# Fewer places for the second products of attention, and a later split of one expert's weights

## The chip, the cores and the metric

The kernel runs on one core of a Trainium2 chip. The metric is the device time of one launch in microseconds (us). TensorE (PE) multiplies, VectorE (DVE), ScalarE (ACT) and GpSimd (POOL) work element by element, and SyncE (SP) issues DMAs. Each engine runs its own instructions in the order in which the program wrote them, and semaphores make it wait for others.

## The reference, cut to what matters

```python
# attention: 4 batches, 8 heads, 576 positions, head size 64, a bias from a small MLP of distances
scores = q @ k.T / 8 + bias                  # softmax over keys
attn   = exp(scores - max) / (sum + 1e-9)
x      = attn @ v                            # 2304 tokens of 512
# dense layer, rational activation
h = x @ w_in                                 # 512 -> 2048
g = (a0 + a1*h + a2*h2 + a3*h3) / (1 + |b0|*|h| + |b1|*h2 + 1e-6)
x = g @ w_out                                # 2048 -> 512
# 8 experts, each token to the best one
e = argmax(x @ w_gate + modality_bias[modality])
out[token] = gate * (relu(x @ w1[e]) @ w2[e])    # 512 -> 1024 -> 512
```

## The kernel before, in words

**Attention.** The work goes by units of one pair of heads and one batch: 16 units of nine steps, 144 steps `g = 9u + j`, in one loop (L524 to L584). A step works on one tile of 128 queries (the ninth takes the 64 left over of both heads) against 576 keys. Its parts are written one after another, each for another tile, so that a tile passes through the loop in about five steps:

- `expo(g-2)` (L351, ACT): the exponentials, with their sum; `recip(g-3)` (L363, L364, DVE, and L366, POOL): the reciprocals of the sums of two tiles;
- the list `pend` (L546 to L548): what copies PSUM of the step before to SBUF, namely `stack_evac` (L302 to L311: the transposed q and k of the next unit), `rest_evac` and `av_evac` (L445, DVE: the result of a unit's second product, times the reciprocals);
- `trans_pe(g-4)` (L393, PE): four transposes of exponentials (L396 and L397 add two in every second step), and `trans_evac` (L370, ACT);
- `scores(g)` (L330, PE): four products of 288 columns (eight in step 8) into one of two PSUM places named sc;
- `stack_pe` (L289 to L294, PE), in steps 0, 1, 2, 3 and 7;
- the second products `attn @ v` (`av_pe`, L436, PE): two output halves (256 and 320 queries), each of five chunks of keys. The tables `AV0` and `AV1` (L520, L521) say at which steps of the next unit they stand: half 0 in steps 0, 1 and 2, half 1 in steps 4, 6, 7 and 8. Each chunk is done on 64 columns of the array for each of the two heads;
- `rowmax(g-1)` (L346, DVE): adds the bias, writes the sum to SBUF and keeps the row's extreme. It frees the PSUM place that `scores(g+1)` writes.

A conversion of the dense layer's weights runs beside it (`CONV`, L516).

**Dense layer.** Six tiles of 384 tokens, each with 16 chunks of the hidden size: 96 iterations G (L1125). In each, PE does 12 first products (L671) and 12 second products (L759, five iterations behind); ACT and DVE compute the rational function of two chunks at a time (L635 to L664). The results of a tile are copied out of PSUM (L766, L768) in the next tile, and its tokens are routed: logits (L775), choice (L785, L787), a chain of small DVE operations (L805 to L853), a place in each expert's table, and three scatters from POOL into tables in DRAM (L863).

**The first expert.** When the last tile begins (G = S1 = 80) the counts of five tiles already name an expert with many tokens. Its weights come as 16 pieces of 128x512. Each piece is loaded (`wa_load`) and split into a high and a low part: a cast on ACT (L937) and a subtraction on POOL (L938). One piece is split in each of the iterations 82 to 97. Behind the last tile (G = 96 to 100) PE does the second products that are left, transposes the rows of 384 early tokens of that expert (`block_x`, L1038) and begins its first products (`split_h`, L1055, eight groups). Then the last tile is copied out and routed, `split_h` goes on, `split_y` (L1076) does the expert's second products, and further rows are gathered by the tables that the last scatters have filled.

The lines that set the order around the change:

```python
AV0 = {0: (0, 1), 1: (2,), 2: (3, 4)}
AV1 = {4: (0, 1), 6: (2,), 7: (3,), 8: (4,)}
i = G - S1 - 2
if 0 <= i < 16:
    wa_tile(i)
    wa_split(i, spec[i], nc.gpsimd)
```

Of the kernel before, what the change touches and what calls it, by code (L numbers as in the profile page):

```python
# [8 lines left out]
F32 = mybir.dt.float32  # L9
F32R = mybir.dt.float32r  # L10
# [4 lines left out]
ALU = mybir.AluOpType  # L15
# [73 lines left out]
def attention(ctx, tc, k, ins):  # L89

    nc = tc.nc
# [5 lines left out]
    pst, xq = k.pst, k.xq  # L97
# [5 lines left out]
    bp = bctx.enter_context(tc.tile_pool(name="bp", bufs=1, side="right"))  # L103
# [336 lines left out]
    def av_evac(u, n):  # L440
        r = units[u]
        w = Q1 if n == 0 else S - Q1
        if n == 0:
            r.xs = ap.tile([P, S], F32, name="xs")
        nc.vector.tensor_tensor(r.xs[:, n * Q1:n * Q1 + w], r.av[:, 0:w], r.aR[n][:, 0], ALU.mult)  # L445
        if n == 1:
            later[g + (3 if u < NU - 1 else 1)] = lambda: nc.sync.dma_start(k.xT[r.p, r.b], r.xs)
# [38 lines left out]
    for s in range(37):  # L486
# [18 lines left out]
        if s in (8, 11, 14, 17, 20):  # L505
            i = (4, 0, 1, 2, 3)[(s - 8) // 3]
# [10 lines left out]
            5: [(1, 1), (8, 0)], 6: [(7, 0), (3, 1), (2, 1), (0, 2)], 7: [(4, 1)], 8: [(5, 1)]}  # L517
    STACK = {0: 4, 1: 0, 2: 1, 3: 2, 7: 3}
    SPLIT = {6: (0,), 7: (1,), 8: (2, 3)}
    AV0 = {0: (0, 1), 1: (2,), 2: (3, 4)}  # L520
    AV1 = {4: (0, 1), 6: (2,), 7: (3,), 8: (4,)}  # L521
    pend = []
    setup = routing_setup(tc, k, ins)
    for g in range(NG + 6):  # L524
        u, j = divmod(g, 9)
# [7 lines left out]
        w, i = divmod(g - 2, 9)  # L533
# [5 lines left out]
            next(setup)  # L539
        if g in later:  # L540
            later[g]()
        if 0 <= g - 3 < NG:
            recip(g - 3)
        if 0 <= g - 2 < NG:
            expo(g - 2)
        for f in pend:  # L546
            f()
        pend = []  # L548
        if 0 <= g - LAG < NG:
            trans_pe(g - LAG)  # L550
            trans_evac(g - LAG)
# [5 lines left out]
        if u + 1 < NU and j in STACK:  # L557
            i = STACK[j]
            ps = stack_pe(u + 1, i)
            pend.append(lambda u=u, i=i, ps=ps: stack_evac(u + 1, i, ps))  # L560
        if 0 <= u - 1 < NU - 1 and j in AV1:
            for c in AV1[j]:
                av_pe(u - 1, 1, c)
            if j == 8:
                pend.append(lambda u=u: av_evac(u - 1, 1))
        if 0 <= g - 1 < NG:
            rowmax(g - 1)
# [3 lines left out]
        v = u - 1  # L571
        if 0 <= v < NU and j in AV0:
            for c in AV0[j]:
                av_pe(v, 0, c)
# [12 lines left out]
        n = g - NG  # L587
# [87 lines left out]
def moe(ctx, tc, k, ins, x2_d, out):  # L675

    nc = tc.nc
# [3 lines left out]
    bp = bctx.enter_context(tc.tile_pool(name="bp1", bufs=2, reuse_waits="tile"))  # L681
    wop = k.persist.enter_context(tc.tile_pool(name="wop", bufs=16, side="right", reuse_waits="tile"))
    pb, xq = k.pst, k.xq
# [184 lines left out]
    w1, w2 = ins["moe2_w1"], ins["moe2_w2"]  # L868
# [51 lines left out]
        k.meta = c0.tile([P, 3, NE], I32, name="meta")  # L920
        nc.vector.tensor_copy(k.meta, mf)

    wa = {}

    def wa_tile(i):
        wa[i] = k.wip.tile([P, 2, DM], F32R, name="w_a", bufs=16)

    def wa_load(i, raw, e):
        if i < 8:
            src = w1[bass.ds(e, 1), (i // 2) * P:(i // 2 + 1) * P, (i % 2) * DM:(i % 2 + 1) * DM]  # L930
        else:
            src = w2[bass.ds(e, 1), (i - 8) * P:(i - 7) * P, :]
        nc.sync.dma_start(raw, src.rearrange("o p n -> (o p) n"))

    def wa_split(i, raw, eng):
        w = wa[i]
        nc.scalar.copy(w[:, 0], raw)  # L937
        eng.tensor_tensor(w[:, 1], raw, w[:, 0].bitcast(F32), ALU.subtract)  # L938


    wsets, rowsets, colsets, halves = [], [], [], []
# [159 lines left out]
            nc.gpsimd.indirect_dma_start(out, bass.IndirectOffsetOnAxis(ap=r.tl[:, a:a + 1].bitcast(U32), axis=0),  # L1101
                                         y, None, bounds_check=NT - 1, oob_is_err=False)

    spec = {}

    def spec_raw(i):

        j = i % 6
        if j == 0:
            a = bp.tile([P, 3, DM], F32, name="x", bufs=1)  # L1110
            k.sraw = [a[:, n] for n in range(3)]
        elif j == 3:
            a = xq.tile([P, 2, DM], F32, name="kn")
            k.sraw = [a[:, n] for n in range(2)]
        elif j == 5:
            k.sraw = [xq.tile([P, DM], F32, name="qn")]
        spec[i] = k.sraw.pop(0)
        wa_load(i, spec[i], k.e0)

    tiles[0] = k.x0  # L1120
    NG = NTT * NF
    FULL = 10
    S1, S0 = NG - NF, NG - NF + 9

    for G in range(NG + 5):  # L1125
        t, f = divmod(G, NF)
# [60 lines left out]
            pick()  # L1187
        if G == S1:
            k.e0 = nc.sync.value_load(k.pick[0:1, 0:1], min_val=0, max_val=NE - 1)
        for i in {1: range(6), 5: (6, 7, 8), 7: (9, 10, 11), 11: (12, 13, 14), 12: (15,)}.get(G - S1, ()):  # L1190
            spec_raw(i)
        i = G - S1 - 2
        if 0 <= i < 16:
            wa_tile(i)
            wa_split(i, spec[i], nc.gpsimd)
        if G == S0 - 1:
            head()
        if G == S0:
# [53 lines left out]
    a = rt.tile([P, 4, NB], F32, name="x2", bufs=1)  # L1252
    for p in range(2):
        c = K()
# [295 lines left out]
```

## Time and profile before

| | us |
|---|---|
| median of three runs | 1071.61 (1068.4 to 1072.78) |
| the profiled execution, its own time | 1070.2 |
| its span, first to last instruction | 1068.4 |
| attention's steps at their steady pace | from about 80 to 375 |
| the dense layer's six tiles | from about 377 to 802 |
| the last tile's end and the first expert's early tokens | about 802 to 870 |

The trace shows every instruction with its start and duration. PE's products overlap, so that a product's duration is longer than the time it costs: what a group costs is read from the start of one group to the start of the next. In brackets stands how long the engine was idle before an instruction, and what ended that.

### The profile page before, as it was taken

The page shows a single profiled execution, that of the slowest core. Times are in us where ns is not written, and L with a number is a line of the kernel's source. Part 1 is how long each engine was busy: PE and PEld are TensorE (multiplying, and loading weights), DVE is VectorE, ACT ScalarE, POOL GpSimd, SP SyncE. Part 2 cuts the span into 40 slices and gives each one's busy share as a digit, 9 for nine tenths or more (in the row PEclk, how much of TensorE's full clock was granted, in tenths as well). Part 3 has the DMA queues.
Part 4 walks back from the last instruction along what each step waited for, and adds up shares of the span by engine and source line. Part 5 has one row for each costly group of instructions (what it writes and reads, how often), then busy time and mean ns, then how long its engine had stood idle before and what let it go on. Part 6 is the DMA issues. An engine that isn't in the chain of part 4 may idle for free. (4 is left out here: it accounts for less than half of the span.)

```text
span 1068.4 us, 19126 instructions
## 1 busy us (share of the span) xinstructions
PE 1017.6 (95%) x6804; PEld 885.4 (83%) x6804; DVE 754.4 (71%) x1544; ACT 651.0 (61%) x1283; POOL 280.8 (26%) x449
## 2 busy tenths in 40 slices
PE   6989999999999999999999999999986999999995
PEld 4667777777777779999999999999885889999983
DVE  7988998888888858898888988888886312111210
ACT  6878778877877857666667766676664222222221
POOL 3433343443443310202112021031253142211210
PEclk9999999999999999999999999999998999999998
DMA  5886885774664236105103031051131256411100
GB/s 170 299 269 165 232 242 182 212 225 128 177 181 116 92 108 260 30 1 30 31 1 38 23 23 38 1 30 60 60 70 30 23 145 230 140 42 40 50 31 18
DMA packets 122074, 113.36 MB, mean 106 GB/s; under 512 B 65055, under 2 KB 94495, under 8 KB 121952
## 3 DMA queue, kind: packets, MB, share of 16 engines
q1 hardware_dynamic: 117828, 101.53, 35.6%
q0 software_dynamic: 3728, 10.25, 3.1%
q8 instruction: 61, 1.00, 0.4%
q14 instruction: 61, 0.50, 0.2%
q10 hardware_dynamic: 396, 0.08, 0.0%
HBM read 78.09 MB, written 33.79 MB: 105 GB/s over the span
## 5 line engine op out<-in xcount | busy, mean ns | idle before, releaser
L759 PE MATMUL sc<-gh,w_b 128*128 128x384 f32 x752 | 209.7, 340 | 3.3 <-ACT x L766 3.3
L759 PEld LDWEIGHTS sc<-gh,w_b 128*128 128x128 f32 x752 | 139.3, 190 | 4.1 <-ACT x L766 3.9
L759 PE MATMUL sc<-gl,w_b 128*128 128x384 f32 x376 | 127.7, 340 | 0.0
L393 PEld LDWEIGHTS tr<-idf,e 128*128 128x128 f32 x576 | 80.5, 207 | 49.3 <-issue 24.9
L351 ACT ACTIVATE e<-e,st 128x576 f32<-128x576 f32 x144 | 112.2, 779 | 13.3 <-DVE st L346 11.4
L370 ACT COPY aT<-tr 128x512 f32<-128x512 f32 x144 | 84.4, 586 | 44.8 <-PE tr L393 42.9
L346 DVE CUSTOM_DVE_ANT_0 e<-sc,bias_s 128x576 f32<-128x576 f32 x144 | 107.6, 748 | 5.4 <-PE sc L330 4.1
L1065 DVE SCALAR_TENSOR_TENSOR hl<-tr,hh 128x256 fp32r<-128x256 f32 x56 | 23.8, 424 | 121.5 <-ACT hh L1064 121.1
L671 PE MATMUL tr<-kn,w_a 128*128 128x384 f32 x372 | 107.3, 343 | 2.1 <-DVE t L642 2.0
L393 PE MATMUL tr<-idf,e 128*128 128x128 f32 x576 | 104.6, 304 | 1.7 <-DVE kk L311 0.9
L330 PE MATMUL sc<-kk,qS 128*128 128x288 f32 x512 | 99.1, 315 | 0.7 <-DVE st L346 0.7
L660 ACT CAST gh<-t 128x768 fp32r<-128x768 f32 x47 | 39.3, 835 | 89.2 <-DVE t L656 89.2
L436 PE MATMUL av<-aT,vn 128*64 128x320 f32 (+1 forms) x512 | 82.8, 424 | 0.0
L1055 PE MATMUL tr<-kn,w_a 128*128 128x256 f32 x448 | 81.6, 280 | 0.9 <-ACT w_b L1100 0.7
L330 PEld LDWEIGHTS sc<-kk,qS 128*128 128x128 f32 x512 | 73.0, 191 | 2.2 <-DVE st L346 1.0
L671 PEld LDWEIGHTS tr<-kn,w_a 128*128 128x128 f32 x372 | 68.0, 188 | 5.7 <-DVE t L642 3.2
L759 PEld LDWEIGHTS sc<-gl,w_b 128*128 128x128 f32 x376 | 71.5, 190 | 0.0
L1055 PEld LDWEIGHTS tr<-kn,w_a 128*128 128x128 f32 x448 | 69.7, 188 | 1.7 <-ACT w_b L1100 1.1
L863 POOL DMA_INDIRECT tab<-ids,si x18 | 21.2, 1178 | 189.7 <-DVE cum L859 167.9
L1076 PE MATMUL sc<-w_a,hh 128*128 128x512 f32 x224 | 70.9, 393 | 0.0
L366 POOL TENSOR_SCALAR rb<-st 128x128 f32<-128x128 f32 x80 | 23.8, 298 | 171.5 <-DVE st L364 154.2
L654 DVE SCALAR_TENSOR_TENSOR t<-t,coef,r 128x768 f32<-128x768 f32 x47 | 49.3, 1048 | 23.9 <-ACT r L650 23.9
(303 smaller groups left out, 2533.2 us busy)
## 6 DMA issues: line engine op xcount, KB each, us to landing
bias_d<-bo SPq DMA_DIRECT2D x36, 295.5 KB, 2.9
kn<-in_k_dram SPq DMA_DIRECT2D x64, 128.0 KB, 3.4
cst<-in_moe_w_out_dram SPq DMA_DIRECT2D x16, 512.0 KB, 4.1
wo_d<-cvw SPq DMA_DIRECT2D x16, 512.0 KB, 2.8
cst<-in_moe_w_in_dram SPq DMA_DIRECT2D x16, 512.0 KB, 4.0
w_b<-wo_d SPq DMA_DIRECT2D x16, 512.0 KB, 6.4
w_b<-in_moe_w_dram SPq DMA_DIRECT2D x16, 512.0 KB, 8.2
x_d<-xr SPq DMA_DIRECT2D x18, 256.5 KB, 9.7
```

Source lines behind the costliest of these rows:

```text
L330: nc.tensor.matmul(ps[:, hf, 0:HF], st, mv[:, hf * HF:(hf + 1) * HF], start=n == 0, stop=n == last)
L346: nc.vector.tensor_tensor_reduce(out=ev, in0=ps[:, :, 0:HF], in1=bv, scale=-1.0, scalar=3.0e38, op0=ALU.add, op1=ALU.min, accum_out=st[:, ...
L351: nc.scalar.activation(e, e, AF.Exp, bias=st[:, 0:1], scale=-1.0, accum_out=st[:, 1:2])
L370: nc.scalar.copy(dst, src)
L393: nc.tensor.transpose(ps[:, c * P:(c + 1) * P], both[:, e0 + c % 2:e0 + 2 * P:2], k.idf)
L436: nc.tensor.matmul(r.av[64 * hd:64 * hd + 64, 0:w], st, mv, start=c == 0, stop=c == 4)
L654: nc.vector.scalar_tensor_tensor(q.t, q.t, co[:, 0:1], q.r, ALU.add, ALU.mult)
L660: self.nc.scalar.copy(gh, q.t)
L671: nc.tensor.matmul(h[:, 0:k.NB], k.wi[f][:, wv, dc * P:(dc + 1) * P], xv[dc], start=n == 0, stop=n == 11)
L759: nc.tensor.matmul(r.acc[dc][:, 0:NB], wo[f][:, wv, ws], gv, start=f == 0 and n == 0, stop=f == NF - 1 and n == 2)
L1055: nc.tensor.matmul(ps[:, 0:n], w[:, wv, cs], xv[dc // 2][:, dc % 2], start=j == 0, stop=j == 11)
L1076: nc.tensor.matmul(r.acc[a], r.h[f][hv][:, cs], wa[8 + f][:, wv], start=f == 0 and n == 0, stop=f == 7 and n == 2)
```

## The change

In attention the second products of a unit stand in four places instead of seven: half 0 in steps 0 (three chunks) and 2 (two), half 1 in steps 4 (two) and 6 (three). The copy `av_evac` of half 1 follows step 6. The list `pend` runs ahead of `recip` and `expo` in each step.

In the dense layer four pieces of the expert are split in iterations 85, 88, 91 and 94, and the other twelve in iterations 98, 99 and 100, four in each, behind the last token tile's products. The order of the pieces is changed so that the four needed by the first four `split_h` come first. Pieces 8 to 15 are loaded into places of the dense layer's second weights, w_b, as these come free, instead of waiting for the places of earlier pieces.

```diff
-    AV0 = {0: (0, 1), 1: (2,), 2: (3, 4)}
-    AV1 = {4: (0, 1), 6: (2,), 7: (3,), 8: (4,)}
+    AV0 = {0: (0, 1, 2), 2: (3, 4)}
+    AV1 = {4: (0, 1), 6: (2, 3, 4)}
...
+        for f in pend:
+            f()
+        pend = []
         if 0 <= g - 3 < NG:
             recip(g - 3)
         if 0 <= g - 2 < NG:
             expo(g - 2)
-        for f in pend:
-            f()
-        pend = []
...
-            if j == 8:
+            if j == 6:
                 pend.append(lambda u=u: av_evac(u - 1, 1))
...
+    def wa_split(i):
+        w = wa[i] = k.wip.tile([P, 2, DM], F32R, name="w_a", bufs=16)
+        nc.scalar.copy(w[:, 0], raw[i])
+        nc.gpsimd.tensor_tensor(w[:, 1], raw[i], w[:, 0].bitcast(F32), ALU.subtract)
...
+    WORD = (0, 2, 4, 6, 1, 3, 5, 7) + tuple(range(8, 16))
+    SPLITS = {5: WORD[0:1], 8: WORD[1:2], 11: WORD[2:3], 14: WORD[3:4], 18: WORD[4:8], 19: WORD[8:12], 20: WORD[12:16]}
...
-        for i in {1: range(6), 5: (6, 7, 8), 7: (9, 10, 11), 11: (12, 13, 14), 12: (15,)}.get(G - S1, ()):
-            spec_raw(i)
-        i = G - S1 - 2
-        if 0 <= i < 16:
-            wa_tile(i)
-            wa_split(i, spec[i], nc.gpsimd)
+        if G == S1 + 1:
+            wa_first()
+        if S1 + 6 <= G < S1 + 10:
+            wa_second(G - S1 - 6)
+        if G == S1 + 12:
+            wa_rest()
+        for i in SPLITS.get(G - S1, ()):
+            wa_split(i)
```

PE in steps 6, 7 and 8 of a unit, before: L393 are the transposes of exponentials, L330 the scores, L291 the transposes of k, L436 the second products (two rows a chunk, one for each head).

```order
L330 MATMUL sc<-kk,qS_1034 128x288 x4
L436 MATMUL av<-aT_1209,vn 64x320 x2
L393 MATMUL tr<-idf,e 128x128 x4
L396 MATMUL av<-idf,e 128x128
L397 MATMUL av<-idf,rb 128x128
L330 MATMUL sc<-kk,qS_1035 128x288 x4
L291 MATMUL tr<-idf,kn 128x128 x4
L436 MATMUL av<-aT_1209,vn 64x320 x2
L393 MATMUL tr<-idf,e 128x128 x4
L330 MATMUL sc<-kk,qrem_119 128x288 x8
L436 MATMUL av<-aR_1210,vrem_117 64x320 x2
L393 MATMUL tr<-idf,e 128x128 x4
```

The same place in the changed kernel:

```order
L330 MATMUL sc<-kk,qS_1034 128x288 x4
L436 MATMUL av<-aT_1209,vn 64x320 x4
L436 MATMUL av<-aR_1210,vrem_117 64x320 x2
L393 MATMUL tr<-idf,e 128x128 x4
L396 MATMUL av<-idf,e 128x128
L397 MATMUL av<-idf,rb 128x128
L330 MATMUL sc<-kk,qS_1035 128x288 x4
L291 MATMUL tr<-idf,kn 128x128 x4
L393 MATMUL tr<-idf,e 128x128 x4
L330 MATMUL sc<-kk,qrem_119 128x288 x8
L393 MATMUL tr<-idf,e 128x128 x4
```

The chunks of steps 7 and 8 stand in step 6, and steps 7 and 8 keep nothing but transposes and scores.

DVE from step 8 to step 0 of the next unit, before: L363 and L364 are the reciprocals, L310 and L311 empty the PSUM of the transposes of k, L346 is `rowmax` (of step 7, then of step 8), L445 the copy of half 1.

```order
L363 TENSOR_SCALAR st<-st 128x2
L364 RECIPROCAL st<-st 128x2
L310 CAST kk<-tr 128x512
L311 TENSOR_TENSOR kk<-tr,kk 128x512
L346 ISA e,st<-sc,bias_s 128x576
L346 ISA st 128x1
L76 CAST cvw<-cvt 128x512
L445 TENSOR_TENSOR xs<-av,aR_1210 128x320
L346 ISA e_1533,st<-sc,bias_s 128x576
```

The same place in the changed kernel:

```order
L310 CAST kk<-tr 128x512
L311 TENSOR_TENSOR kk<-tr,kk 128x512
L363 TENSOR_SCALAR st<-st 128x2
L364 RECIPROCAL st<-st 128x2
L346 ISA e,st<-sc,bias_s 128x576
L346 ISA st 128x1
L76 CAST cvw<-cvt 128x512
L346 ISA e_1536,st<-sc,bias_s 128x576
```

The reciprocals stand between the emptying of PSUM and `rowmax`, and L445 is gone from here (it stands in step 7).

ACT behind the last token tile, before: L1041 copies the transposed early rows, L1064 is the ReLU of `split_h`, L937 a piece's cast, L766 the copy of the last tile out of PSUM.

```order
L1041 CAST w_b<-av 128x384
L1064 ACTIVATE w_b<-tr 128x384
L937 CAST w_a<-kn 128x512
L1064 ACTIVATE w_b<-tr 128x384
L766 COPY x_9942<-sc 128x384 x2
```

The same place in the changed kernel (its lines are numbered 1063, 1086, 936 and 767):

```order
L1063 CAST w_b<-av 128x384
L1086 ACTIVATE w_b<-tr 128x384 x2
L936 CAST w_a<-kn 128x512
L936 CAST w_a<-qn 128x512
L936 CAST w_a<-x 128x512 x2
L936 CAST w_a<-w_b 128x512 x8
L767 COPY x_9942<-sc 128x384 x2
```

Twelve casts stand ahead of the last tile's copy, and on POOL the twelve subtractions stand in the same way ahead of the last tile's three scatters.

## Rows read from the trace of the kernel before

**Rows 1.** Busy time by stretch: PE, PEld, DVE, ACT, POOL, clock, DMA, GB/s.

```profile
200.00:225.00 25.00, 25.00 (x187) 19.22 (x186) 21.98 (x62) 20.65 (x47) 9.21 (x20) 1.00 0.74 221
```

**Rows 2.** Timeline of PE, steps 0 to 4 of a unit: start, duration, instruction.

```profile
199.92 0.77 PE L330 MATMUL sc<-kk,qS 128*128 128x288 f32 x4
...
200.79 1.08 PE L436 MATMUL av<-aT,vn 128*64 128x256 f32 x8
...
202.31 0.77 PE L330 MATMUL sc<-kk,qS 128*128 128x288 f32 x4
...
203.31 0.65 PE L436 MATMUL av<-aT,vn 128*64 128x256 f32 x4
...
204.61 0.77 PE L330 MATMUL sc<-kk,qS 128*128 128x288 f32 x4
...
207.27 0.77 PE L330 MATMUL sc<-kk,qS 128*128 128x288 f32 x4
...
208.86 0.77 PE L330 MATMUL sc<-kk,qS 128*128 128x288 f32 x4
```

**Rows 3.** Timeline of PE, the scores of steps 5 to 8 and 0.

```profile
211.51 0.77 PE L330 MATMUL sc<-kk,qS 128*128 128x288 f32 x4
...
212.51 0.77 PE L330 MATMUL sc<-kk,qS 128*128 128x288 f32 x4
...
214.62 0.77 PE L330 MATMUL sc<-kk,qS 128*128 128x288 f32 x4
...
216.96 1.30 PE L330 MATMUL sc<-kk,qrem 128*128 128x288 f32 x8
...
219.60 0.77 PE L330 MATMUL sc<-kk,qS 128*128 128x288 f32 x4
```

**Rows 4.** Timeline of DVE in the same unit, steps 4 and 8.

```profile
208.53 0.16 DVE L363 TENSOR_SCALAR st<-st 128x2 f32<-128x2 f32 x1
...
208.81 0.74 DVE L346 CUSTOM_DVE_ANT_0 e<-sc,bias_s 128x576 f32<-128x576 f32 x1
...
215.87 0.69 DVE L310 CAST kk<-tr 128x512 fp32r<-128x512 f32 x1 [0.62 <-PE tr L291]
...
217.20 0.75 DVE L346 CUSTOM_DVE_ANT_0 e<-sc,bias_s 128x576 f32<-128x576 f32 x1
```

**Rows 5.** Timeline of PE, first product of iterations 68, 79, 84 and 95.

```profile
672.38 0.34 PE L671 MATMUL tr<-kn,w_a 128*128 128x384 f32 x1
...
721.67 0.34 PE L671 MATMUL av<-kn,w_a 128*128 128x384 f32 x1
...
742.74 0.34 PE L671 MATMUL tr<-kn,w_a 128*128 128x384 f32 x1
...
800.33 0.44 PE L671 MATMUL tr<-kn,w_a 128*128 128x384 f32 x1 [1.17 <-DVE t L642]
```

**Rows 6.** PE's groups by line, 800 to 823.3 us: busy, mean ns, idle before.

```profile
L1055 PE MATMUL tr<-w_b,w_a 128*128 128x384 f32 x12 | 3.5, 416 | 4.1 <-ACT w_b L1041 3.7 <-DVE w_b L1042 0.4
L1038 PE MATMUL av<-idf,qs 128*128 128x128 f32 x8 | 1.9, 300 | 3.8 <-DVE w_b L1042 2.5 <-DVE t L642 1.1
```

**Rows 7.** Timeline of DVE in iteration 97.

```profile
815.97 2.11 DVE L654 SCALAR_TENSOR_TENSOR t<-t,coef,r 128x768 f32<-128x768 f32 x1
818.12 1.02 DVE L655 SCALAR_TENSOR_TENSOR r<-q,one,r 128x768 f32<-128x768 f32 x1
```

**Rows 8.** Groups of the split pieces on ACT and POOL, 735 to 830 us.

```profile
L937 ACT CAST w_a<-x 128x512 fp32r<-128x512 f32 x9 | 5.6, 617 | 0.0
...
L938 POOL TENSOR_TENSOR w_a<-x,w_a 128x512 fp32r<-128x512 f32 x9 | 13.6, 1516 | 36.8 <-ACT w_a L937 29.5 <-PE av L1038 4.0 <-PE sc L759 3.3
```

**Rows 9.** Timeline of PE and POOL behind the last tile.

```profile
833.61 2.26 PE L1055 MATMUL tr<-w_b,w_a 128*128 128x384 f32 x12
...
843.96 1.01 POOL L863 DMA_INDIRECT tab<-ids,si  x1 [18.05 <-DVE count L856]
...
866.20 0.98 PE L1038 MATMUL av<-idf,xg 128*128 128x128 f32 x7 [1.05 <-DMA xg<-x_d,tixg]
```

More of the change, by code (lines that the diff above doesn't have):

```diff
@@ L921, in order, with wa_load, wa_first, wa_rest @@
         nc.vector.tensor_copy(k.meta, mf)
[L923 to L928, printed above, removed]
+    wa, raw = {}, {}
+    def wa_load(i, place):
         if i < 8:
-            src = w1[bass.ds(e, 1), (i // 2) * P:(i // 2 + 1) * P, (i % 2) * DM:(i % 2 + 1) * DM]
+            src = w1[bass.ds(k.e0, 1), (i // 2) * P:(i // 2 + 1) * P, (i % 2) * DM:(i % 2 + 1) * DM]
         else:
[L932 to L938, printed above, removed]
+            src = w2[bass.ds(k.e0, 1), (i - 8) * P:(i - 7) * P, :]
+        raw[i] = place
+        nc.sync.dma_start(place, src.rearrange("o p n -> (o p) n"))
+    def wa_split(i):
+        w = wa[i] = k.wip.tile([P, 2, DM], F32R, name="w_a", bufs=16)
+        nc.scalar.copy(w[:, 0], raw[i])
+        nc.gpsimd.tensor_tensor(w[:, 1], raw[i], w[:, 0].bitcast(F32), ALU.subtract)
+    def wa_first():
+        a = bp.tile([P, 3, DM], F32, name="x", bufs=1)
+        b = xq.tile([P, 2, DM], F32, name="kn")
+        c = xq.tile([P, DM], F32, name="qn")
+        for i, place in zip(WORD, (a[:, 0], a[:, 1], a[:, 2], b[:, 0], b[:, 1], c)):
+            wa_load(i, place)
+    def wa_rest():
+        a = bp.tile([P, 3, DM], F32, name="x", bufs=1)
+        for n in range(2):
+            wa_load(WORD[6 + n], a[:, n])
+    def wa_second(n):
+        a = wop.tile([P, 2, DM], F32, name="w_b", bufs=16)
+        for j in range(2):
+            wa_load(8 + 2 * n + j, a[:, j])
+    WORD = (0, 2, 4, 6, 1, 3, 5, 7) + tuple(range(8, 16))
+    SPLITS = {5: WORD[0:1], 8: WORD[1:2], 11: WORD[2:3], 14: WORD[3:4], 18: WORD[4:8], 19: WORD[8:12], 20: WORD[12:16]}
     wsets, rowsets, colsets, halves = [], [], [], []
@@ L1102, in block_out @@
                                          y, None, bounds_check=NT - 1, oob_is_err=False)
[L1104 to L1118, printed above, removed]
     tiles[0] = k.x0
```

## The prediction

> **What bounds the kernel now.** I read the busy time by stretch first. In a steady stretch of attention PE is never idle, DVE is busy for 21.98 of 25 us and ACT for 20.65 [rows 1]. PE being busy proves little, since its products overlap, so I went on to PE's timeline of one unit and took times from start to start. From the scores of step 0 to those of the next unit's step 0 it takes 219.60 - 199.92 = 19.68 us [rows 2, 3], and most units repeat this. In these rows hardly any group of PE waits for a semaphore: it is PE's order that costs time, and what to look for is which of its entries cost more than their columns. In the dense layer I compared the last tile with the one before, iteration by iteration, on PE; then I read who ended PE's waits behind it, and last the way from the final scatters to the rows that they let PE have.
>
> **Attention: the price of a place.** A chunk of 256 columns costs 1.08 - 0.65 = 0.43 us (two chunks against one in a place) [rows 2]; one of 320 columns I take as 0.43 x 320/256 = 0.54.
> - Step 1. Scores to scores takes 2.30 us with one chunk in between (202.31 to 204.61) and 1.59 us in step 3, where the same transposes stand without a chunk (207.27 to 208.86) [rows 2]. The place costs 0.71, its chunk 0.43, so 0.28 is the price of entering and leaving.
> - Step 7. Without a chunk and without other transposes the interval is 1.00 (211.51 to 212.51) [rows 3]. Step 3's 1.59 exceeds this by 0.59 for six transposes, of which the four of the stack get 0.43. Step 7 takes 2.34 (214.62 to 216.96) [rows 3]: 2.34 - 1.00 - 0.43 - 0.54 = 0.37.
> - Step 8. It takes 2.64 (216.96 to 219.60) [rows 3]. Four more score products are half of the 1.00, two transposes the remaining 0.16 to 0.20 of the 0.59: 2.64 - 1.00 - 0.50 - 0.20 - 0.54 = 0.40.
>
> Three places less are worth 0.28 + 0.37 + 0.40 = 1.05, taken as 1.0 us a unit for PE. The chunks that move add no boundary where they go, since a place stands there already.
>
> **What is late next.** Scores of step 0 need the PSUM place that `rowmax` of step 7 frees. In the trace that `rowmax` ends at 217.20 + 0.75 = 217.95, and the scores start at 219.60: 1.65 us to spare [rows 3, 4]. `rowmax` cannot come earlier, because it stands behind L310, and L310 waits for PE's transposes of k in step 7 (0.62 us idle before it) [rows 4]. From those transposes on PE loses the chunks of steps 7 and 8 with their boundaries, 2 x 0.54 + 0.37 + 0.40 = 1.85. The new order also puts the reciprocals between L311 and `rowmax`, 0.28 (208.53 to 208.81) [rows 4]. So 1.65 - 1.85 - 0.28 = -0.48: PE waits about 0.45 in step 0 of each unit. Elsewhere I find nothing late: L445 leaves step 0, and steps 0 and 6 grow by 0.43 and 1.08 for the others to catch up. ACT gets its PSUM copies ahead of the exponentials; in 19.7 us it idles 3.4 (4.35 of 25) [rows 1], and a copy made sooner also frees the place of PE's transposes sooner. The result's DMA follows L445 by three steps as before, on an SP queue with nothing urgent behind it. A wait on SP or POOL is not added.
>
> 15 units lose 1.0, 14 pay 0.45: 15.0 - 6.3 = **8.7 us**. The ends: 15 (no new wait) and 0 (DVE takes everything).
>
> **The last tile.** Iterations 84 to 95 take 800.33 - 742.74 = 57.6 us; the same stretch of the tile before takes 721.67 - 672.38 = 49.3 [rows 5]. The 8.3 us more go with the 16 splits. A subtraction on POOL holds up a DVE operation that has two inputs in SBUF: L654 took 2.11 where the next, of the same size, took 1.02 [rows 7]. With four splits in place of fourteen up to iteration 95, about 0.9 of such a delay falls on every three iterations, within what DVE idles. I let 0.9 of the 8.3 stay (the counts and the `head` chain are still there): 7.4 gained; ends 4 and 8.3.
>
> From 800 to 823.3 PE idles 4.1 + 3.8 = 7.9 us before the early rows' transposes and the first `split_h` [rows 6]. This is one chain through ACT and DVE for the last pair of chunks; three subtractions lengthen it by 1.09 each and three casts by 0.5 each (0.617 [rows 8], overlapping its neighbour), 4.8 together. That much I take off; ends 0 and 7.9. 7.4 + 4.8 = 12.2 us by which the second products of the last tile end sooner.
>
> **What the moved splits cost.** Call M the end of these products (833.61 before [rows 9]). Two groups of twelve products stand between the second `split_h` and M, an iteration's worth, so the casts begin at about M - 4. Twelve take 12 x 0.52 = 6.2, to M + 2.2; two copies of the last tile follow on ACT, 0.8, and the logits, which PE had at M + 2.2 (behind `split_h`), begin at M + 3.4: 1.2 late. The subtractions take 12 x 1.5 = 18 [rows 8], from M - 3.5 to M + 14.5. Meanwhile the routing chain has five operations with two inputs in SBUF; each can lose between nothing and a whole subtraction, 1.5, and I take 0.72, 3.6 together. The scatters were issued at 843.96 = M + 10.35 [rows 9]; now they need the chain, M + 10.35 + 1.2 + 3.6 = M + 15.2, and POOL free at M + 14.5. So they are issued 4.8 late against M. The rows that hang on them released PE 866.20 - 843.96 = 22.2 us after the first scatter [rows 9], and PE had only just come to wait for them (1.05 idle). So PE goes on 4.8 later against M, and this stretch gains 12.2 - 4.8 = **7.4 us**. The ends: 0 lost (12.2) and 10 lost (2.2: the subtractions at 2 us each, as much as the DVE operation beside one took [rows 7]).
>
> The Trainium skill, page "SBUF — State Buffer", section "Who interferes with whom", says that a DVE instruction with two SBUF inputs contends with a GpSimd instruction that reads SBUF, and that the loser fully blocks until the other ends. The row of 2.11 us agrees. By the rule alone each of the five operations would lose nearly a whole subtraction, 7.2 us instead of 3.6, and the time would be 3.6 higher; this is the third rival.
>
> Pieces 1, 3, 5 and 7 are needed by the fifth `split_h`, behind logits and two groups of products, some 6 us after M, and are split by M + 2.5; pieces 8 to 15 by M + 14.5, their first product comes after M + 17. Their loads wait only for places that PE has left five iterations before.
>
> **Sum.** 1070.2 - 8.7 - 7.4 = 1054.1 by the profiled execution's own time (its span is 1068.4). The median of the runs shown is 1.4 higher, 1071.61; so 1055.5, taken as 1055.
>
> **The rivals.**
> 1. DVE does not become late: PE keeps the whole 15 us. For it: 1.65 us to spare where I count 2.13 as used, so a small error decides; against it: L310's wait, which ties `rowmax` to PE's own transposes. 1055.5 - 6.3 = 1049.
> 2. The boundary's price goes with the chunks and not with the place, so that attention gains nothing and the change does not do what it says there. For it: that price rests on differences between steps; against it: three steps give 0.28 to 0.40. 1055.5 + 8.7 = 1064.
> 3. POOL's queue: subtractions of 2 us and a routing chain blocked in full. Scatters then wait until M + 20 or more. 1055.5 + 5 = 1060.5.
> 4. The other side: ACT. Three times in a unit a copy of the stack now stands ahead of an exponential. If ACT has run ahead of PE, that copy is not ready and ACT waits for up to a step, 2.30 [rows 2], where it did an exponential before. 3 x 2.30 = 6.9, less 3.4 that ACT idles anyway, less the 1.0 gained: +2.5 a unit, 15 x 2.5 - 7.4 = +30, so 1102. It decides once ACT loses more than 3.4 + 1.0 + 0.5 a unit. Against it: ACT's copies already follow PE's step closely, and the exponentials have two steps before they are needed.
>
> **Chances.** The forecast 0.58, rival 1 0.14, rival 2 0.08, rival 3 0.16, rival 4 0.04. The range: the forecast's own, from the ends of its terms, is about 1050 to 1060; with rivals 1 and 3 and part of 2 it is 1046 to 1063. Half a per cent (5.4 us) is about what a measurement of this kernel can tell from no change. Forecast and rivals 1 and 3 lie beyond it on the fast side, rival 2 too, but close: faster 0.91, same 0.05, slower 0.04.
>
> **What would show it.** In attention: four groups of second products a unit; score intervals of 1.6 in step 1, 1.4 in step 7 and 1.8 in step 8; a unit of 19.1 to 19.2 us; in step 0 a PE that waits 0.4 to 0.5 for `rowmax`. 18.7 would be rival 1, 19.7 rival 2, ACT busy without a gap and units over 20 rival 4. In the dense layer: the last tile's iterations at the pace of the tile before; a PE idle of about 3 us in place of 7.9 behind it; twelve casts in a row ahead of L766's copy; scatters some 15 us after the end of the second products; PE waiting again before the transposes of gathered rows. I am wrong in the main if the unit's length does not fall below 19.4, or if the scatters come no sooner than before.

## Result and profile after

The changed kernel takes 1083.18 us (median, 1082.04 to 1086.29), the kernel before, run beside it, 1070.57 (1068.4 to 1072.78): ratio 1.0125, 95% interval 1.01 to 1.015. It is slower by 12.6 us where 1055 was forecast. The profiled execution has a span of 1081.6 us at a mean granted clock of 0.990 of full speed.

The loss lies in attention alone. Iteration 66 of the dense layer starts at 683.12 us instead of 664.03, 19.1 later; from there to the end the changed kernel is 5.9 us shorter. First the stretch of attention that answers to [rows 1]: PE, which had no gap, now has 1.5 us of gaps in 25. DVE and ACT are busy for a smaller share, but a unit takes longer: in a steady unit DVE is busy for 18.42 us of 21.20, where it was 16.89 of 19.68.

```profile
200.00:225.00 25.00, 23.52 (x174) 18.30 (x174) 21.08 (x53) 19.35 (x45) 10.51 (x19) 1.00 0.67 206
```

Next, PE's timeline of the changed kernel from step 7 of one unit to step 1 of the next; it answers to [rows 2, 3], with columns as there.

```profile
226.22 0.77 PE L330 MATMUL sc<-kk,qS 128*128 128x288 f32 x4
...
227.67 1.31 PE L330 MATMUL sc<-kk,qrem 128*128 128x288 f32 x8
...
229.88 0.79 PE L330 MATMUL sc<-kk,qS 128*128 128x288 f32 x4
...
231.38 0.28 PE L294 MATMUL tr<-idr,qs 128*128 128x128 f32 x1 [0.59 <-POOL qs L268]
231.59 1.51 PE L436 MATMUL av<-aT,vn 128*64 128x256 f32 x12
...
233.53 0.77 PE L330 MATMUL sc<-kk,qS 128*128 128x288 f32 x4
234.37 0.54 PE L289 MATMUL tr<-idr,qs 128*128 128x128 f32 x4
235.62 0.75 PE L393 MATMUL tr<-idf,e 128*128 128x128 f32 x4 [0.70 <-ACT aT L370]
```

Read from scores to scores, as in the prediction, a steady unit looks like this (us; "forecast" is the sum of the prediction's terms for each step). Of the 14 units that follow the first, 12 take 21.12 to 21.26 and two 21.60 and 23.48; in the kernel before ten take 19.68 and four 20.17 to 20.77.

| step | 0 | 1 | 2 | 3 | 4 | 5 | 6 | 7 | 8 | unit |
|---|---|---|---|---|---|---|---|---|---|---|
| before | 2.39 | 2.30 | 2.65 | 1.59 | 2.65 | 1.00 | 2.12 | 2.34 | 2.64 | 19.68 |
| forecast | 2.82 | 1.59 | 2.65 | 1.59 | 2.65 | 1.00 | 3.20 | 1.43 | 2.25 | 19.18 |
| after | 3.65 | 2.81 | 2.66 | 1.59 | 2.65 | 1.00 | 3.19 | 1.44 | 2.21 | 21.20 |

Seven of the nine steps came out within 0.04. Steps 0 and 1 are 0.83 and 1.22 too long, and that is the whole miss in a steady unit. The bracketed waits in PE's rows name two releasers: in step 0 POOL's split of q (L268, the part of the split that PE's transposes L294 read), in step 1 ACT's copy of the transposed exponentials (L370). POOL's timeline of the changed kernel at that place:

```profile
229.32 0.30 POOL L366 TENSOR_SCALAR rb<-st 128x128 f32<-128x128 f32 x1 [4.57 <-DVE st L364]
229.58 1.74 POOL L268 TENSOR_TENSOR qs<-qt,qs 128x320 fp32r<-128x320 f32 x2
231.28 0.73 POOL L78 TENSOR_TENSOR cvw<-cvt,cvw 128x256 fp32r<-128x256 f32 x1
```

POOL had nothing to do for 4.57 us, because the broadcast of the reciprocals (L366) stood at the head of its queue and waited for DVE; the two pieces of q's split (L268), for which nothing was missing, stood behind it and ended 0.06 before PE's L294 started. DVE's timeline of the same stretch shows why L366 was late and what followed:

```profile
227.47 0.69 DVE L310 CAST kk<-tr 128x512 fp32r<-128x512 f32 x1
...
229.00 0.17 DVE L364 RECIPROCAL st<-st 128x2 f32<-128x2 f32 x1
229.08 0.74 DVE L346 CUSTOM_DVE_ANT_0 e<-sc,bias_s 128x576 f32<-128x576 f32 x1
...
229.74 0.99 DVE L76 CAST cvw<-cvt 128x512 fp32r<-128x512 f32 x1
...
231.33 0.97 DVE L61 TENSOR_SCALAR cvt<-cst 128x512 uint32<-128x512 uint32 x1
232.33 1.11 DVE L62 SCALAR_TENSOR_TENSOR cvt<-cst,cvt 128x512 uint32<-128x512 uint32 x1
...
233.67 0.29 DVE L303 TENSOR_TENSOR kk<-tr,kk 128x128 fp32r<-128x128 f32 x1
```

The rows answer to [rows 4]: the reciprocal now stands behind both copies of k's stack. L76 and L61 take more than twice the 0.42 us that each takes before, with POOL's displaced L268 and L78 running beside them; with L62 (1.11 in place of 0.69) that is the 1.5 us that DVE is busy for longer in a unit. The small stack (the transposes of the last 64 keys and queries, step 0) is copied by L302 and L303, last in this queue; they are late, and with them ACT, whose timeline closes the chain:

```profile
234.06 0.27 ACT L305 CAST qrem<-tr 128x128 fp32r<-128x128 f32 x1 [2.28 <-DVE st L363]
234.22 0.78 ACT L351 ACTIVATE e<-e,st 128x576 f32<-128x576 f32 x1
...
234.99 0.57 ACT L370 COPY aT<-tr 128x512 f32<-128x512 f32 x1
```

ACT idles 2.28 us in front of L305. This copy empties the same PSUM place as L303 and waits for it (the row names the DVE instruction behind L303; in the kernel before, all 16 waits in front of L305 end with L303). Behind it in ACT's queue stands an exponential that could have run, since its `rowmax` had ended by 231.4; the copy L370, for which PE waits, comes behind both. In the kernel before, the exponential stood ahead of L305.

Behind attention, the rows that answer to [rows 5, 9] (PE and POOL; first products of iterations 84 and 95, the end of the last tile's second products, the first scatter, the gathered rows):

```profile
761.95 0.34 PE L672 MATMUL tr<-kn,w_a 128*128 128x384 f32 x1
...
812.26 0.34 PE L672 MATMUL tr<-kn,w_a 128*128 128x384 f32 x1
...
841.80 2.26 PE L1077 MATMUL tr<-w_b,w_a 128*128 128x384 f32 x12
...
853.95 0.18 PE L838 MATMUL av<-ohb,lower 128*128 128x8 bf16 x1 [2.69 <-DVE ohb L817]
...
856.39 1.01 POOL L864 DMA_INDIRECT tab<-ids,si  x1 [2.54 <-DVE count L857]
...
878.85 1.12 PE L1060 MATMUL av<-idf,xg 128*128 128x128 f32 x8
```

Iterations 84 to 95 take 50.31 us (57.6 before), from iteration 95 to the end of the products it is 29.54 (33.28), from there to the scatter 14.59 (10.35). The gathered rows are transposed 22.5 us behind the scatter, without a wait. PE's groups from iteration 95 to the end of the products, which answer to [rows 6], show 2.9 + 2.3 = 5.2 us of idle time in place of 7.9:

```profile
L1077 PE MATMUL tr<-w_b,w_a 128*128 128x384 f32 x26 | 5.7, 351 | 2.9 <-ACT w_b L1063 2.3 <-DVE w_b L1064 0.6
L1060 PE MATMUL av<-idf,qs 128*128 128x128 f32 x8 | 1.9, 323 | 2.3 <-DVE t L643 1.5 <-DVE w_b L1064 0.8
```

### The profile page after: what moved, and what is told of

It is laid out like the page before. It is cut to its first block, busy times and chain, and to the rows that moved or that the text cites. A ratio compares the mean times of both kernels' runs of the same rounds, so it can differ in the third digit from the quotient of the medians.

```text
span 1081.6 us, 19063 instructions
## 1 busy us (share of the span) xinstructions
PE 1018.1 (94%) x6804; PEld 891.8 (82%) x6804; DVE 770.7 (71%) x1544; ACT 646.1 (60%) x1283; POOL 284.1 (26%) x449
## 5 line engine op out<-in xcount | busy, mean ns | idle before, releaser
L393 PEld LDWEIGHTS tr<-idf,e 128*128 128x128 f32 x576 | 81.0, 206 | 39.8 <-ACT aT L370 19.2
L346 DVE CUSTOM_DVE_ANT_0 e<-sc,bias_s 128x576 f32<-128x576 f32 x144 | 107.4, 746 | 5.9 <-PE sc L330 4.9
L393 PE MATMUL tr<-idf,e 128*128 128x128 f32 x576 | 101.1, 298 | 10.7 <-ACT aT L370 9.8
L370 ACT COPY aT<-tr 128x512 f32<-128x512 f32 x144 | 83.6, 580 | 34.0 <-PE tr L393 32.4
L330 PE MATMUL sc<-kk,qS 128*128 128x288 f32 x512 | 99.5, 316 | 0.5 <-DVE st L346 0.4
L436 PE MATMUL av<-aT,vn 128*64 128x320 f32 (+1 forms) x512 | 76.4, 420 | 0.0
L330 PEld LDWEIGHTS sc<-kk,qS 128*128 128x128 f32 x512 | 72.9, 191 | 3.2 <-DVE st L346 0.7
L366 POOL TENSOR_SCALAR rb<-st 128x128 f32<-128x128 f32 x80 | 23.8, 297 | 174.8 <-DVE st L364 161.3
```

The lines of the kernel that those rows point to most:

```text
L330: nc.tensor.matmul(ps[:, hf, 0:HF], st, mv[:, hf * HF:(hf + 1) * HF], start=n == 0, stop=n == last)
L346: nc.vector.tensor_tensor_reduce(out=ev, in0=ps[:, :, 0:HF], in1=bv, scale=-1.0, scalar=3.0e38, op0=ALU.add, op1=ALU.min, accum_out=st[:, ...
L370: nc.scalar.copy(dst, src)
L393: nc.tensor.transpose(ps[:, c * P:(c + 1) * P], both[:, e0 + c % 2:e0 + 2 * P:2], k.idf)
L436: nc.tensor.matmul(r.av[64 * hd:64 * hd + 64, 0:w], st, mv, start=c == 0, stop=c == 4)
```

## Experiments

Theory: the fewer places are worth what was forecast, and the new order of the emptying gives it back through three queues: POOL (split of q behind the late broadcast, step 0), ACT (exponential behind a copy that is not ready, step 1), DVE (small stack's copies late, step 1). Rival: the fuller places of steps 0 and 6 themselves make PE late. Each run was timed beside the kernel before on the same chip, so across groups the ratio is what compares; it has its 95% interval, and the columns at the right are steady units of the profile (us).

| run | median | before | ratio | unit | step 0 | step 1 | step 8 |
|---|---|---|---|---|---|---|---|
| later splits alone | 1064.73 | 1069.77 | 0.9949 [0.9933, 0.9965] | 19.68 | 2.39 | 2.30 | 2.64 |
| places alone | 1067.08 | 1069.77 | 0.997 [0.9959, 0.9981] | 19.55 | 2.84 | 2.09 | 2.04 |
| emptying first alone | 1078.34 | 1069.77 | 1.0077 [1.0063, 1.0091] | 20.14 | 2.39 | 2.75 | 2.64 |
| after, reciprocals first | 1071.93 | 1069.77 | 1.0018 [1.0008, 1.0027] | 20.27 | 2.84 | 2.86 | 2.04 |
| places and later splits | 1059.81 | 1071.09 | 0.9899 [0.9883, 0.9914] | 19.54 | 2.85 | 2.09 | 2.04 |
| + conversion shifted | 1061.82 | 1071.09 | 0.991 [0.9895, 0.9924] | 19.36 | 2.84 | 1.64 | 2.04 |
| after, q split early | 1072.47 | 1071.09 | 1.0022 [1.0007, 1.0037] | 20.17 | 2.84 | 2.58 | 2.22 |
| + q split early | 1064.28 | 1071.09 | 0.9938 [0.9925, 0.9951] | 19.55 | 2.84 | 2.10 | 2.04 |
| + small stack early | 1062.55 | 1069.92 | 0.9939 [0.9924, 0.9953] | 19.70 | 2.85 | 1.73 | 2.04 |
| + small stack early, rowmax first | 1061.16 | 1069.92 | 0.9917 [0.9903, 0.993] | 19.57 | 2.82 | 1.91 | 1.75 |
| + small stack early, emptying before exponentials | 1061.48 | 1069.92 | 0.9917 [0.9903, 0.9931] | 19.45 | 2.84 | 1.73 | 2.04 |
| + one cast on ACT | 1056.47 | 1071.8 | 0.9855 [0.9833, 0.9878] | 19.10 | 2.84 | 1.67 | 2.04 |

"+" stands for "places and later splits" with one edit more.

### Which part loses

Later splits alone (attention as before).

> Attention as in the kernel before, the later splits as in the changed kernel. Theory: the two parts are independent, attention lost all that was lost and the later splits gained about what the two traces show between the start of tile iteration 64 and the end, 19.1 - 13.2 = 5.9 us. So units of 19.68 us and about 1064.7 us (1063 to 1067). Rival: the later splits give less than that because the half-clock stretches around 820 to 835 us lie elsewhere in this run; then 1068 to 1071. As the prediction had it (7.4 gained) it would be 1063.

It fell on the expected number: units of 19.68, 5.0 us faster than the kernel before. So the later splits lose nothing.

Places alone:

```diff
-    AV0 = {0: (0, 1), 1: (2,), 2: (3, 4)}
-    AV1 = {4: (0, 1), 6: (2,), 7: (3,), 8: (4,)}
+    AV0 = {0: (0, 1, 2), 2: (3, 4)}
+    AV1 = {4: (0, 1), 6: (2, 3, 4)}
...
-            if j == 8:
+            if j == 6:
                 pend.append(lambda u=u: av_evac(u - 1, 1))
```

> Only the places of the second products change (four in a unit); the emptying of PSUM stays behind the reciprocals and the exponentials, and the splits of the weights stay where they were. Theory: the loss comes from the emptying put first, because it holds back the reciprocals on DVE, with them the broadcast on POOL and the splits of q queued behind it. Then the places alone gain about 0.8 to 1.0 us in a unit: step 1 takes 1.6 us, step 7 1.4, step 8 1.8 to 2.0, step 0 about 2.9, a unit 18.7 to 18.9, and the time is 1056 to 1059. Rival: the fuller places of steps 0 and 6 themselves make PE wait, in whatever order the others stand; then units of 20.5 us and more and a time over 1080.

Faster, so the rival falls; but by 2.7 us and not by 11 to 14. Step 1 took 2.09 us, not 1.6. PE of this run, from the scores of step 0 to those of step 2:

```profile
217.70 0.80 PE L330 MATMUL sc<-kk,qS 128*128 128x288 f32 x4
...
220.54 0.77 PE L330 MATMUL sc<-kk,qS 128*128 128x288 f32 x4
221.42 0.53 PE L289 MATMUL tr<-idr,qs 128*128 128x128 f32 x4
221.91 0.75 PE L393 MATMUL tr<-idf,e 128*128 128x128 f32 x4
...
222.63 0.38 PE L330 MATMUL sc<-kk,qS 128*128 128x288 f32 x1
```

L289 starts 0.05 behind the end of ACT's L305 (221.37) and L393 0.05 behind the end of the copy after it; L305 had waited 0.73 us for DVE's L303. DVE's timeline in this run shows the conversion (L62, 0.69 in the kernel before) ahead of the small stack, and POOL's part of the conversion beside it:

```profile
218.75 0.91 POOL L80 TENSOR_TENSOR cvw<-cvt,cvw 128x256 fp32r<-128x256 f32 x1
219.12 1.10 DVE L62 SCALAR_TENSOR_TENSOR cvt<-cst,cvt 128x512 uint32<-128x512 uint32 x1
...
220.72 0.29 DVE L303 TENSOR_TENSOR kk<-tr,kk 128x128 fp32r<-128x128 f32 x1
```

So a part of the loss, 0.50 us a unit (2.09 against 1.59), belongs to the places and not to the order: PE got faster than DVE follows. Of this lateness 0.41 us is as much as L62 takes longer beside L80; no run takes that stretch away with the order of the copies as it is, so how the 0.50 divide between DVE's own work and its neighbour on POOL stays open. (In the last run below L62 stays stretched, at 1.10, and step 1 still falls to 1.67 when other work leaves DVE.)

Emptying first alone:

```diff
+        for f in pend:
+            f()
+        pend = []
         if 0 <= g - 3 < NG:
             recip(g - 3)
         if 0 <= g - 2 < NG:
             expo(g - 2)
-        for f in pend:
-            f()
-        pend = []
```

> Only the emptying of PSUM is put ahead of the reciprocals and exponentials; seven places of second products as before, the splits of the weights as before. Theory: the reciprocal of step 5 then stands behind a wait of DVE for PE's transposes of step 7 and comes some 2.4 us later, and POOL's splits of q with it; as steps 7 and 8 still have their products, the transposes of q in step 0 come late enough for that, and a unit gets 0 to 0.6 us longer: 1071 to 1080. Rival: the emptying put first costs by itself what the changed kernel lost and more (it also lacks the gain of the places): units of 22 us, about 1105.

8.6 us slower, units 0.46 longer, all of it in step 1; step 0 stays at 2.39 in most units. As expected, with the long steps 7 and 8 the split of q is still in time. That the time fell into the expected range is partly luck: what costs here is step 1, where PE's L393 waits behind the same exponential on ACT, and the theory did not name it.

### The two halves of the new order

The changed kernel with the reciprocals ahead of the emptying, which stays ahead of the exponentials:

> The changed kernel with the reciprocals put back ahead of the emptying of PSUM, which still stands ahead of the exponentials. Theory: the reciprocals behind the emptying are the cause, through POOL's queue (broadcast, then splits of q). Then step 0 takes 2.8 to 3.0 us and step 1 1.6 to 1.8, a unit 18.7 to 19.1, and the time is 1050 to 1057. Rival: ACT's order is the cause (copies that are not ready stand ahead of exponentials); then steps 0 and 1 stay at 3.6 and 2.8, and the time at 1083.

Part of it came: 1071.93, not 1050 to 1057. Step 0 fell from 3.65 to 2.84 and step 8 from 2.21 to 2.04; step 1 stayed at 2.86, and so the rival has its part as well. ACT and PE of this run in step 1:

```profile
227.70 0.27 ACT L305 CAST qrem<-tr 128x128 fp32r<-128x128 f32 x1 [1.50 <-DVE kk L303]
227.87 0.78 ACT L351 ACTIVATE e<-e,st 128x576 f32<-128x576 f32 x1
...
228.64 0.57 ACT L370 COPY aT<-tr 128x512 f32<-128x512 f32 x1
```

```profile
229.27 0.74 PE L393 MATMUL tr<-idf,e 128*128 128x128 f32 x4 [0.71 <-ACT aT L370]
```

Places alone differs from this run, in attention, only in where the exponentials stand. There L370 followed L305 at once; here the exponential between them makes 2.86 out of 2.09: 0.77 us, the time of one exponential.

The changed kernel with `SPLIT` one step earlier, {5: (0,), 6: (1,), 7: (2, 3)}, so that L268 stands ahead of the late L366:

> The changed kernel as it is, with the splits of q on POOL one step earlier in the program (steps 5, 6 and 7 in place of 6, 7 and 8), so that they stand ahead of the broadcast of the late reciprocals in POOL's queue. Theory: step 0 grew by 0.8 us because PE's transpose of q's last chunk waits for those splits; then step 0 takes 2.8 to 3.0 us, a unit 20.3 to 20.5, and the time is 1070 to 1074. Rival: DVE's own order (reciprocals behind the long copies) holds step 0 up whatever POOL does; then step 0 stays at 3.5 us and the time at 1080 to 1084.

As the theory said: step 0 is 2.84 and the unit 20.17. POOL and PE of this run:

```profile
218.67 1.86 POOL L268 TENSOR_TENSOR qs<-qt,qs 128x320 fp32r<-128x320 f32 x2
223.83 0.30 POOL L366 TENSOR_SCALAR rb<-st 128x128 f32<-128x128 f32 x1 [3.29 <-DVE st L364]
```

```profile
224.39 0.80 PE L330 MATMUL sc<-kk,qS 128*128 128x288 f32 x4
...
225.05 0.30 PE L294 MATMUL tr<-idr,qs 128*128 128x128 f32 x1
...
227.23 0.77 PE L330 MATMUL sc<-kk,qS 128*128 128x288 f32 x4
```

L366 comes as late as before against the scores (0.56 us ahead of them in both runs), and L294 no longer waits. The 0.81 us are the queue's order on POOL. Step 1 fell as well, from 2.81 to 2.58: with L268 done before the scores, L76 and L61 take 0.42 and 0.52 us in place of 0.99 and 0.97, and the small stack's copies come sooner. So part of step 1 hung on POOL's queue too.

### Both good parts together, and what holds them

The changed kernel with the old order of the emptying:

> The changed kernel with the emptying of PSUM put back behind reciprocals and exponentials; four places a unit and the later splits stay. Theory: the two parts add, 1067.1 + 1064.7 - 1069.8 = 1062.0 us (1060 to 1064), units of 19.55 us. Rival: they share a limit (the loads of the first expert's weights, or the half-clock stretches behind the last tile), then one of the two gains is lost and the time is 1064.5 to 1067.

The parts add, 0.2 us better than the expected range; it is faster than both kernels. From here I tried to win step 1 back.

```diff
-    CONV = {0: [(6, -1), (8, -1), (1, 0), (2, 0)], 1: [(3, 0), (7, -1), (0, 1)], 2: [(4, 0)], 3: [(5, 0)], 4: [(6, 0)],
-            5: [(1, 1), (8, 0)], 6: [(7, 0), (3, 1), (2, 1), (0, 2)], 7: [(4, 1)], 8: [(5, 1)]}
+    CONV = {0: [(5, -1)], 1: [(6, -1), (8, -1)], 2: [(7, -1), (1, 0), (2, 0), (3, 0), (0, 1)], 3: [(4, 0)], 4: [(5, 0)],
+            5: [(6, 0)], 6: [(8, 0), (7, 0), (1, 1), (2, 1)], 7: [(3, 1), (0, 2)], 8: [(4, 1)]}
```

> As the run with places and later splits, and the conversion of the dense weights is shifted on DVE: its first operations of a unit from step 0 to step 2, the others by one or two steps. Theory: with four places DVE is behind from step 5 to step 1 (it is busy without a gap there), its copy of the small stack comes 1.8 us after the transposes are there, and PE waits for it in step 1 (2.09 instead of 1.59) and for the rowmax of step 7 in step 0. With 1.6 us of conversion out of that stretch step 1 takes 1.6 to 1.7 us, a unit 18.9 to 19.2, and the time is 1052 to 1058. Rival: the wait of step 1 is ACT's, which copies the stack behind an exponential; then step 1 stays at 2.0 and more and the time at 1062. Third: the shifted conversion makes DVE late in steps 2 to 4 instead; then those intervals grow and the time is 1062 or more.

Step 1 fell to 1.64, so DVE's conversion is what held it; but step 3 grew from 1.59 to 1.88, the first unit by 0.75 and single units by 0.5 to 1.3 over the steady one, and the time is no better. The theory of step 1 holds, and so does the third case, that DVE becomes late elsewhere.

With the splits of q early:

> The run with places and later splits, with the splits of q one step earlier as well. Theory: they do not hold up anything there (the reciprocals stand ahead of the copies), and what stretches the DVE operations of step 0 (1.10 us for one that takes 0.69 alone) is POOL's part of the conversion, which stays; so the time stays at 1060 to 1063, step 1 at 2.0 to 2.1. Rival: it is the splits that stretch them; then step 1 falls to 1.7 and the time to 1056 to 1058.

Steps 0, 1 and 8 are unchanged, as expected, but the time is 1.3 us above the expected range. One unit of 22.73 shows what the move cost (POOL, then PE):

```profile
236.30 0.67 POOL L263 TENSOR_SCALAR qt<-qn 128x576 f32<-128x576 f32 x1 [5.23 <-DMA qn<-in_q_dram]
```

```profile
238.42 0.33 PE L397 MATMUL av<-idf,rb 128*128 128x128 f32 x1 [1.57 <-POOL rb L366]
```

The split now waits for q's load at the head of POOL's queue, with the broadcast behind it.

The small stack emptied in step 0, ahead of the conversion, with DVE's work the same:

```diff
+        if j == 0:
+            for f in pend:
+                f()
+            pend = []
         for part, d in CONV[j]:
```

> As the run with places and later splits, and the small stack of step 0 (DVE's two short copies, ACT's copy, POOL's) is emptied in step 0 itself, ahead of the conversion's operations, in place of step 1. DVE does the same work in another order. Theory: PE's waits in step 1 are the end of one chain, DVE's conversion, then the small stack's copies, then ACT's; with the copies ahead of the conversion step 1 takes 1.6 to 1.7 in place of 2.09 us, a unit 19.05 to 19.15, and the time is 1051 to 1056 (1059.8 - 14 x 0.45 = 1053.5). Rival: DVE is full from step 5 to step 1, so whatever is put last there is late: step 1 or step 2 grows by as much, a unit stays at 19.5 and the time at 1059 to 1061.

Step 1 did almost as the theory says (1.73), the unit (19.70) and the time did as the rival says, the time 1.6 us above its range: step 2 grew from 2.69 to 3.21. There PE waits for the next stack of q, which ACT copies behind an exponential that started late (ACT and PE):

```profile
205.17 0.60 ACT L307 CAST qS<-tr 128x512 fp32r<-128x512 f32 x1
...
205.82 0.66 PE L291 MATMUL tr<-idf,kn 128*128 128x128 f32 x4 [0.34 <-ACT qS L307]
```

In the next run the emptying of step 8 stands behind `rowmax(g - 1)`:

> As the run with the small stack early, and in step 8 the rowmax of step 7 stands on DVE ahead of the two copies of k's stack, not behind them. Theory: PE's scores of step 0 wait for this rowmax; ahead of the copies it ends 1.4 us sooner, step 8 takes 1.80 in place of 2.04 us, and a unit gets 0.24 us shorter: 1048 to 1052. Rival: the copies, 0.75 us later, free their PSUM place late for the transposes of steps 8 and 0, and the 0.24 us are lost there again or more: 1053 to 1060.

Step 8 went to 1.75 (1.80 expected), step 1 gave back 0.18 of the 0.29: theory and rival share it. The time, 1061.16, lies above both ranges, since both start from the 1051 to 1056 expected of the run before, and step 2 kept its 3.2.

The run with the small stack early, and the emptying ahead of the exponentials:

> As the run with the small stack early, and the emptying of PSUM ahead of the exponentials (still behind the reciprocals), as in the changed kernel. Theory: the 0.71 us a unit that this order cost was one place, step 1, where ACT's copy of the small stack waited for DVE with an exponential queued behind it; with that copy done in step 0 the order costs nothing, and the time is that of the run with the small stack early within 2 us. Rival: a copy ahead of an exponential costs at the other two stacks of q as well; then a unit is 0.3 us longer or more, and the time 4 to 10 us above.

The time is the same within 1.1 us. With the small stack out of step 1, the order that had cost 0.72 us a unit (20.27 against 19.55) gains 0.25: the price was that one blocked copy (L305), not the copies of the other two stacks of q. Step 2 is back at 2.66, and step 3 has grown to 1.89; the wait moves on.

Last, work taken off DVE in place of a new order:

```diff
-            nc.vector.tensor_copy(c.w[:, 0], c.t.bitcast(F32))
+            if i % 2:
+                nc.scalar.copy(c.w[:, 0], c.t.bitcast(F32))
+            else:
+                nc.vector.tensor_copy(c.w[:, 0], c.t.bitcast(F32))
```

> As the run with places and later splits, and one copy of the conversion, the cast of every second piece in step 8 (0.42 us on DVE), is given to ACT, which idles about 1 us there, waiting for the rowmax of step 7. Theory: with four places DVE's load from step 5 to step 3 is what keeps PE waiting, so only work taken off DVE, not work put in another order on it, is not given back later. L302 then comes 0.4 us sooner, step 1 takes 1.65 to 1.75 us in place of 2.09 and step 2 stays at 2.7; a unit takes 19.1 to 19.2 and the time is 1053 to 1056. Rival: the wait moves as it did when the order was changed (step 2 or 3 grows by what step 1 loses), or ACT's 0.6 us delays its exponentials; then a unit stays at 19.4 to 19.6 and the time at 1058 to 1062.

Step 1 is 1.67, step 2 stays at 2.67, the unit is 19.10, and the time is 1056.47, half a microsecond above the expected range and the best of all. ACT does the cast (L77) in a gap and still waits for the rowmax behind it (ACT's timeline; line numbers are three higher from L77 on):

```profile
214.06 0.64 ACT L77 CAST cvw<-cvt 128x512 fp32r<-128x512 f32 x1
215.26 0.78 ACT L354 ACTIVATE e<-e,st 128x576 f32<-128x576 f32 x1 [0.57 <-DVE st L349]
```

The edit saves 0.4 us on DVE and 0.44 in the unit. The median is 3.3 us lower and not 14 x 0.44 = 6.2; by the ratios, each beside its own kernel before, it is 4.7.

## Why the prediction was wrong

**The price of a place: right.** Steps 6 and 7 hit the forecast within 0.01. In the run with the cast on ACT, where step 1 is nearly free of waits, it takes 1.67 (1.59 forecast). With steps 0, 6 and 7 from places alone, step 1 from the cast on ACT and step 8 from the rowmax first, the change of places is worth 0.45 - 0.63 + 1.07 - 0.90 - 0.89 = -0.90 (-1.0 forecast); this is a sum over three runs, and no single run shows it whole. Rival 2 falls: where the chunks went, steps 0 and 6 grew by 0.45 and 1.07, the chunks' own 0.43 and 1.08.

**The new wait for `rowmax` of step 7: right.** Step 8 takes 2.21 where 1.80 + 0.45 = 2.25 was forecast. Without the reciprocals between it is 2.04, and with the rowmax ahead of the copies 1.75.

**"Elsewhere I find nothing late": the step that failed.** The prediction worked out the slack of one consumer (the scores behind `rowmax`) and put the others behind the same two moves at nothing. Three were late:

- Step 0, +0.81: "a wait on SP or POOL is not added" was wrong. No wait was added to POOL's list, but the one that heads its queue, L366 on the reciprocal, was moved: the reciprocal (L364) starts 1.53 us behind L310 instead of 0.78 ahead of it, by the same reorder for which 0.28 was charged, and q's split stood behind it. The runs with reciprocals first and with q's split early both take this away.
- Step 1, +0.50: DVE's queue from k's stack to the small stack. Places alone has it, and shifting, reordering or removing DVE's work changes step 1 (from 2.09 to 1.64, 1.73, 1.67).
- Step 1, +0.77: an exponential behind a copy that is not ready. This is rival 4's mechanism, at one place in the unit and not at three, and for the time of one exponential. "ACT's copies already follow PE's step closely" did not hold for the one that waits for DVE.

Together 2.08 over the 19.18 of the forecast: 21.26, measured 21.20. The three come from runs in which the other two are absent or changed, so they need not add up as closely as they do. In the sum, -8.7 became +19.1. Of rival 4's two signs one came (units over 20), the other not: ACT was not busy without a gap, it idled in front of the copy.

**The last tile and the moved splits: right in mechanism, near in size.** Iterations 84 to 95 gained 7.3 (7.4 forecast), the stretch behind them 3.7 (4.8), the scatter came 4.2 later (4.8). The logits are 1.3 late (1.2), and the routing chain lost 2.9 (3.6). The subtractions were priced too high (1.28 us each, not 1.5, so that they end 12.1 behind M and not 14.5), which cost nothing, since the scatters waited for the chain. Wrong was that PE would wait for the gathered rows again: it reaches them late by itself, held 2.69 by the routing chain and slowed by a stretch at half clock (856.1 to 859.5), and the balance of this part (all behind attention) is -5.9 in this trace, -5.4 between the spans of later splits alone and the kernel before, and -7.1 between those of the runs with places, for a forecast of -7.4.

The 7.3 us of iterations 84 to 95 are made of two things that the prediction did not separate. PE idled 5.7 us there and now 0.7; the longest wait was for ACT's copy of the tile, behind DVE operations stretched beside the subtractions:

```profile
751.80 0.45 PE L759 MATMUL sc<-gh,w_b 128*128 128x384 f32 x1 [2.62 <-ACT x L766]
```

The other 2.2 us are products that take less time. Right behind this wait, from 752.5 to 755.9, PE ran at a granted clock of 0.50 (1.2 GHz). The three kernels with the early splits each have such a stretch of 3.4 us in these iterations, the eleven with the later splits have none there: with the waits the time at half clock went as well.

## What to carry to other kernels

When a reorder moves an instruction behind a wait, list what stands behind its consumers in their in-order queues, on every engine, and work out the slack of each; the first consumer found late was here one of four. An instruction that is ready should not be queued behind one that waits, even where the waiting one is more urgent. When PE is made faster, an engine that was busy for 88% of the time (DVE here, 21.98 of 25 us) can become the next limit. A new order on it then mostly moved the wait to another step; what paid was work moved to an engine with a gap at that place.

## What the hardware showed

Very short operations pay for a neighbour as much as long ones. In the routing chain beside POOL's eight subtractions in a row, operations of 24 columns that take 0.18 us each in the kernel before take up to 1.21, about one subtraction (1.28), and a plain cast is among them (POOL, then DVE of the changed kernel):

```profile
843.94 9.92 POOL L937 TENSOR_TENSOR w_a<-w_b,w_a 128x512 fp32r<-128x512 f32 x8
...
849.94 0.27 DVE L810 TENSOR_TENSOR oh<-lg,mx 128x24 f32<-128x24 f32 x1
850.25 1.21 DVE L811 TENSOR_TENSOR oh<-oh,er 128x24 f32<-128x24 f32 x1
851.49 0.18 DVE L813 TENSOR_REDUCE m<-oh 128x3 f32<-128x24 f32 x1
851.70 0.97 DVE L814 TENSOR_TENSOR oh<-oh,m 128x24 f32<-128x24 f32 x1
852.71 1.18 DVE L817 CAST ohb<-oh 128x24 bf16<-128x24 f32 x1
```

Each stretched operation ends 0.03 to 0.04 us behind the end of one of the subtractions (851.42, 852.64, 853.86). The reductions between them (L813, and L806 with 0.18) keep their length beside the same subtractions, and so does L788 (0.17), one of whose two inputs lies in PSUM.

The prediction reckoned with operations of two inputs only; L817, L76 and L61, all stretched, have one. The Trainium skill, page "SBUF — State Buffer", section "Who interferes with whom", says that casts and tensor_scalar in a two-port mode take the port pair that DVE and GpSimd share, for the whole instruction; L61 with 0.97 in place of 0.42 agrees. In which mode it ran, no row here shows.

Behind PE's waits for the last tile's chain and its `split_h` the granted clock fell to half (1.2 in place of 2.4 GHz) for 3.4 or 6.8 us in all, at places that differ from kernel to kernel. In the kernels with the later splits the stretch from iteration 95 to the end of the second products took 28.0 us with 3.4 at half clock that began 10.5 after its start, 29.4 to 29.5 with 3.4 that began 19 after it, and 29.5 to 30.8 with 6.8. Single profiles of kernels with the same tail differ by 1 to 3 us there.
